# Attention and gated feed-forward on one core: tiles turned one step earlier, query in three parts, normalizing and weight searches at fixed steps, peak sums in the output bank

## Chip, cores, metric

One core of a Trainium2 chip. The time is device time in microseconds (us), lower is better. The engines are TensorE (PE), VectorE (DVE), ScalarE (ACT), GpSimd (POOL) and SyncE (SP); each works through its own queue in order, and they wait for each other by semaphores.

## What is computed

```python
def _A_ref(x, k_cache, v_cache, wq, wo):       # 32 query heads, 16 key/value heads, Dh = 128
    q = (x @ wq).reshape(B, Sq, Hq, Dh).transpose(0, 2, 1, 3)
    k = jnp.repeat(k_cache[:, :, Sk - W:, :], rep, axis=1)    # W = 512, rep = 2
    v = jnp.repeat(v_cache[:, :, Sk - W:, :], rep, axis=1)
    p = _softmax(jnp.einsum("bhqd,bhkd->bhqk", q, k) * (Dh ** -0.5))
    o = jnp.einsum("bhqk,bhkd->bhqd", p, v)
    return o.transpose(0, 2, 1, 3).reshape(B, Sq, Hq * Dh) @ wo
def _B_ref(x, w1, w3, w2):                     # x: 2048 x 576, F = 4608
    return (_silu(x @ w1) * (x @ w3)) @ w2
...
h = _layernorm(x) * (1 + ca) + sa;  x = x + ga * _A_ref(h, ...)
h = _layernorm(x) * (1 + cb) + sb;  x = x + gb * _B_ref(h, ...)
```

The six vectors sa, ca, ga, sb, cb, gb are the parts of silu(c) @ w_mod.

## The kernel before

The order of the instructions on each engine is the order in which the program writes them down; nothing reorders them.

**Slots and steps.** Attention is cut into 128 slots: one query head with one block of 512 rows. Two slots in turn, of the two query heads of one key/value head, form a pair. A key/value head is one "use" of 8 slots (all four blocks) or, for the first three and the last six heads, two uses of 4 slots each, the second of which loads the split weights, keys and values that the first has stored. A slot has four steps, one for each 128 rows. The main loop (L1201 on) runs over slots `i` and steps `t` and writes down, for each step:

- `turn(i - 1, t)` (L406): four PE transposes of a 128 x 512 tile of exponentials into one of two PSUM banks "T", and ACT's copy of the high half into `ptw` (L415);
- `scores(i, t)` (L371): three matmuls (high and low halves in 16 bits), DVE's maximum (L382) and its scaling (L383), then `turn_low(i - 1, t)` (L417, L420, DVE, low half of the turned tile, which frees the bank), then ACT's exponential (L389);
- `sums(i - 1, t)` (L392): the reciprocals of the row sums at step 0, their store to DRAM at step 1, their load, spread over the partitions (`r`), at step 2; store and load are issued by ACT's queue;
- `query(i + 1, t)` (L359): a part of the 14 query matmuls of the next slot; with the last quarter ACT and DVE split the result (L368, L369);
- `attend_out` pieces (L448): six output matmuls into `E`, a tile of two PSUM banks of which 288 columns each are used (L337), and with every second piece DVE's accumulation into `acc` (L453). A pair's eight pieces fill the two slots that begin one slot behind the values of its second slot;
- the tasks that `at` and `step_at` have put down for this step.

Behind step 3 stands `values(i - 1)` (L424): twelve matmuls into `po` (L432), which need all four turned tiles; then, at once, DVE's normalizing with `r` (L436) into `on`, ACT's copy (L445) and POOL's difference (L446).

**Preparing a head.** For each new use, the tasks (L962 on) load keys, values and query weights, search the largest magnitude of each with DVE (`find_peak`, L234), add the peaks over the partitions with one PE matmul against ones and take the powers of two from the sum with DVE (`sum_peaks`, L241; `powers`, L227, its lines 230 to 232), and scale and split them (`split_in` L260, `turn_k` L295, `split_v` L288, `split_out` L277). `sum_peaks` takes one of the two "T" banks. R is the first step of the use; loads are put at R - 22 and R - 21, searches at R - 17 and R - 16, sums at R - 14, splits at R - 13 to R - 11.

**Work for the second stage.** Between slots 13 and 106, POOL and ACT form sums of the feed-forward weights and store them (`make_set` L592, `make_rows` L646, loads `load_raw` L579 and `load_rows` L629, all on SP's queue). Three more modulation vectors are made at slots 14, 20 and 23. From slot 106 on the second layer norm of the first two blocks is formed and stored, read back, combined and stored again as operands of the feed-forward products (`store_h`, `combine`, `load_set` L554). The feed-forward stage, a generator `mlp`, is interleaved with the last slots from slot 127 on and then runs alone: PE multiplies sums of weights with sums of rows (L685) and the results with w2 (L770).

**Buffers.** A pool has a number of buffers for each tag: "T", "A", "S" two PSUM banks each (turned tiles, query and values, scores), `E` one; in SBUF "p" 4, "raw" 3 (raw query weights), "qh" and "ql" 1 each, "kv" 8, "hs" 7, "w" 8, "o" 3.

## Time and profile before

| | us |
|---|---|
| runs | 3148.26, 3139.47, 3142.55 |
| median | 3142.55 |
| profiled execution | 3128.98 |
| its span, first to last instruction | 3127.2 |
| mean granted PE clock in the span | 0.987 |

The profile is of one execution. Busy time of an engine is the time in which one of its instructions ran; matmuls are pipelined, so PE counts as busy also where it runs below its pace. In a timeline row the first number is the start, the second the duration, both in us; x4 joins four instructions; a bracket gives the idle time ahead and what ended it. In a row of waits stand the engine and line that waited, what for, the total, the number of times and the longest.

### The profile page before, as it was taken

How to read it: one execution, taken by the hardware profiler on the slowest of the kernel's cores; microseconds unless marked ns; L12 is line 12 of the kernel's file. 1: busy time of each engine (PE TensorE's matmuls, PEld its weight loads, DVE VectorE, ACT ScalarE, POOL GpSimd, SP SyncE). 2: the span in 40 equal slices, each digit the busy share in tenths (PEclk: the TensorE clock that was granted, in tenths of full speed). 3: DMA queues.
4: the chain of work that ended last, by engine and by line, in shares of the span. 5: the costliest groups of instructions: out<-in, count | busy, mean ns of one | idle time of the engine just before them, and what ended most of it. 6: DMA issues, size and time to landing. Idle time of an engine off the chain costs nothing.

```text
span 3127.2 us, 48547 instructions
## 1 busy us (share of the span) xinstructions
PE 2970.0 (95%) x16952; PEld 2131.3 (68%) x16952; DVE 2050.2 (66%) x3519; ACT 1514.8 (48%) x3077; POOL 1595.2 (51%) x1667
## 2 busy tenths in 40 slices
PE   6899899999999999998999999999999999999999
PEld 3455455555555555555565557888888888888887
DVE  7677567767777777777787666655555555555556
ACT  4566556666666666666655553333333222222222
POOL 2225566666666666666621342435556355343345
PEclk8999899999999999999999999999999999999999
DMA  4325555555555555665632465666766676666664
GB/s 145 104 78 158 161 159 168 157 168 157 158 163 156 161 154 172 213 202 168 211 105 69 143 222 183 202 225 239 247 230 234 229 260 224 198 199 205 195 200 147
DMA packets 336180, 560.53 MB, mean 179 GB/s; under 512 B 51904, under 2 KB 144064, under 8 KB 334144
## 3 DMA queue, kind: packets, MB, share of 16 engines
q1 hardware_dynamic: 298464, 523.59, 50.5%
q10 hardware_dynamic: 37472, 33.84, 4.6%
q8 instruction: 135, 2.21, 0.3%
q14 instruction: 109, 0.89, 0.1%
HBM read 390.92 MB, written 166.36 MB: 178 GB/s over the span
## 4 chain that ended last, share of the span: by engine, by line
PE 66%; DVE 10%; ACT 6%; DMA 6%; POOL 6%; issue 4%; SPq 1%; ACTq 0%; POOLq 0%; DVEq 0%
PE py L685 15%; PE px L685 11%; PE po L432 7%; PE pe L770 6%; PE pf L770 6%; PE pe L337 5%; PE pss L379 5%; PE pq L326 4%; PE pt L414 4%; DVE ptw L420 2%; DVE nm L382 2%; DMA row<-l 2%; ACT ptw L415 2%; DVE on L436 2%; DMA wraw<-in_B_w 1%
## 5 line engine op out<-in xcount | busy, mean ns | idle before, releaser
L389 ACT ACTIVATE p<-pss,nm,factors 128x512 f32<-128x512 f32 x512 | 396.5, 774 | 240.6 <-DVE nm L383 239.5
L685 PE MATMUL py<-hset,wset 128*128 128x512 f32 x2016 | 507.8, 391 | 0.0
L337 PE MATMUL pe<-o 128*128 128x288 f16 x3072 | 459.3, 286 | 17.6 <-DVE acc L453 17.6
L420 DVE SCALAR_TENSOR_TENSOR ptw<-pt,ptw 128x512 f16<-128x512 f32 x512 | 351.1, 686 | 167.7 <-ACT ptw L415 167.5
L382 DVE TENSOR_REDUCE nm<-pss 128x1 f32<-128x512 f32 x512 | 352.0, 688 | 144.6 <-PE pss L379 144.1
L337 PEld LDWEIGHTS <-o 128*128 128x128 f16 x3072 | 299.6, 98 | 194.9 <-issue 33.1
L432 PE MATMUL po<-ptw,v 128*128 128x512 f16 x1536 | 370.2, 386 | 57.7 <-ACT ptw L415 49.2
L379 PE MATMUL pss<-k,qT 128*128 128x512 f16 x1536 | 420.8, 383 | 2.4 <-ACT p L389 1.6
L685 PEld LDWEIGHTS py<-hset,wset 128*128 128x128 f32 x2016 | 362.5, 188 | 59.2
L685 PE MATMUL px<-hset,wset 128*128 128x512 f32 x1512 | 381.0, 391 | 0.0
L414 PE MATMUL pt<-ident,p 128*128 128x128 f32 x2048 | 312.9, 276 | 40.6 <-DVE us L230 28.0
L446 POOL TENSOR_TENSOR o<-on,o 128x512 f16<-128x512 f32 x128 | 148.4, 1159 | 375.0 <-ACT o L445 364.0
L415 ACT ACTIVATE ptw<-pt 128x512 f16<-128x512 f32 x512 | 303.9, 594 | 37.8 <-PE pt L414 27.7
L432 PEld LDWEIGHTS <-v 128*128 128x128 f16 x1536 | 151.8, 99 | 238.2 <-issue 92.5
L685 PEld LDWEIGHTS px<-hset,wset 128*128 128x128 f32 x1512 | 275.5, 188 | 50.0 <-ACT p L389 0.3
L414 PEld LDWEIGHTS pt<-ident,p 128*128 128x128 f32 x2048 | 247.7, 142 | 81.2 <-issue 25.3
L90 POOL TENSOR_TENSOR akv<-u,akv 128x512 fp32r<-128x512 f32 x141 | 181.3, 1294 | 234.8 <-ACT akv L89 232.7
L326 PE MATMUL pq<-hT,wq 128*128 128x512 f16 x1092 | 299.0, 383 | 0.0
L445 ACT CAST o<-on 128x512 f16<-128x512 f32 x128 | 79.1, 618 | 347.9 <-DVE on L436 347.9
L605 POOL TENSOR_TENSOR wmade<-wraw,wmade 128x256 fp32r<-128x256 f32 x252 | 185.2, 735 | 105.0 <-issue 52.0
L453 DVE SCALAR_TENSOR_TENSOR acc<-pe,factors,acc 128x576 f32<-128x576 f32 x256 | 206.9, 808 | 7.3 <-PE pe L337 7.0
L326 PEld LDWEIGHTS <-wq 128*128 128x128 f16 x1104 | 109.3, 99 | 139.6 <-issue 10.3
(186 smaller groups left out, 4907.8 us busy)
## 6 DMA issues: line engine op xcount, KB each, us to landing
oset<-od SPq DMA_DIRECT2D x106, 576.0 KB, 4.8
od<-omade SPq DMA_DIRECT2D x133, 288.0 KB, 3.3
r<-row ACTq DMA_DIRECT2D x128, 256.0 KB, 3.8
wraw<-in_B_w SPq DMA_DIRECT2D x144, 128.0 KB, 2.7
w2raw<-in_B_w SPq DMA_DIRECT2D x38, 288.0 KB, 4.0
oset<-od SPq DMA_DIRECT2D x35, 288.0 KB, 3.3
oraw<-in_A_wo SPq DMA_DIRECT2D x16, 576.0 KB, 6.3
wraw<-in_B_w SPq DMA_DIRECT2D x288, 32.0 KB, 2.4
```

The costliest lines, as they stand in the source:

```text
L326: nc.tensor.matmul(ps, w[:, k // 2, m, :], hT[:, DC + m if k == 1 else m, :], start=s == 0, stop=False)
L337: nc.tensor.matmul(E[:, h, :HALF], o[:, x, rows], w[:, y, h * HALF : (h + 1) * HALF], start=first and n == 0, stop=last and n == 2,)
L379: nc.tensor.matmul(pss, q[:, x, rows], k[:, y, :], start=n == 0, stop=n == 2)
L382: nc.vector.tensor_reduce(nm[:, 0:1], pss, axis=AX.X, op=ALU.max, negate=True)
L389: nc.scalar.activation(p, pss, AF.Exp, bias=nm[:, 1:2], scale=factor, accum_out=st["l"][:, t : t + 1])
L414: nc.tensor.transpose(ps[:, j, :], p[:, j * P : (j + 1) * P], ident)
L415: nc.scalar.activation(st["pt"][:, 0, :, t * P : (t + 1) * P], st["t"], AF.Copy, scale=P_UP)
L420: nc.vector.scalar_tensor_tensor(pt[:, 1, :, cols], state[i]["t"], P_UP, pt[:, 0, :, cols], op0=ALU.mult, op1=ALU.subtract)
L432: nc.tensor.matmul(po, v[:, x, c, :], pt[:, y, c, :], start=c == 0 and n == 0, stop=c == KC - 1 and n == 2)
L453: nc.vector.scalar_tensor_tensor(a, E[:, :, :HALF], factors[:, uses[u][0], 2:3], a, op0=ALU.mult, op1=ALU.add)
L685: nc.tensor.matmul(ps, w[:, a, :], h[:, b, :], start=start and n == 0, stop=stop and n == 6, skip_group_check=True)
L770: nc.tensor.matmul(ps[:, h, :HALF], a[:, rows], w[:, b, :], start=m == 0, stop=m == 2)
```

## The change

- Step `t` of slot `i` turns tile `t + 1` of slot `i - 1`; step 3 turns tile 0 of slot `i` itself. The low half follows behind the scores' maximum, the exponential (now `weights`) behind that.
- The 14 query matmuls are written down as 5, 5 and 4 in steps 0 to 2; the split query takes the tags "qh" and "ql" in turn.
- `values` ends with its matmuls. Normalizing is written down in step 0 of the next slot but one of its own (`normalize(i - 2)`), behind `weights`; copy and difference in step 1 (`split_on`). `on` takes a buffer of "raw".
- The load of `r` stands at the end of step 2, behind that step's tasks.
- Output pieces stand two steps later; those of the last two pairs four and three to a step.
- The sum matmul writes columns 400 to 415 of the second bank of `E`, ahead of the step's output pieces (`("pre", t)`); the reading of the sums (`scales`) is a task of its own one step later.
- The tasks of a head are spread: loads at R - 22 to R - 18, searches at R - 17 and R - 13, sums at R - 10, scales at R - 9, splits at R - 8, R - 4, R - 5 and R - 1; output weights are loaded at R - 3, split at R + 11 and R + 13.
- Weight sums run from slot 16 to 107, loads of w2 rows and their first task two steps earlier; the second layer norm and what follows it one slot later; operands of the products three steps later; two modulation vectors at slots 105 and 108 instead of 20 and 23.

```diff
     def sum_peaks(g, lo, hi, ps=None):
-        ps = t_bank() if ps is None else ps
+        ps = E[:, 1, 400:416] if ps is None else ps
+        nc.tensor.matmul(ps[:, lo:hi], ones, peaks[g][:, lo:hi], start=True, stop=True)
+
+    def scales(g, lo, hi, ps=None):
+        ps = E[:, 1, 400:416] if ps is None else ps
         small = peaks[g]
-        nc.tensor.matmul(ps[:, lo:hi], ones, small[:, lo:hi], start=True, stop=True)
         powers(small, ps, lo, hi, 5, 2.0**-14)
...
-    QP = (range(0, 3), range(3, 6), range(6, 9), range(9, 14))
+    QP = (range(0, 5), range(5, 10), range(10, 14))
...
-            q = st["qT"] = pool.tile([P, 2, SB], F16, tag="qh", name="qT", bufs=QB)
+            q = st["qT"] = pool.tile([P, 2, SB], F16, tag=("qh", "ql")[i % 2], name="qT", bufs=QB)
...
-        on = pool.tile([P, SB], F32, tag="ql", name="on", bufs=QB)
+        st["po"] = po
+
+    def normalize(i):
+        st = state[i]
+        po = st.pop("po")
+        on = st["on"] = pool.tile([P, SB], F32, tag="raw", name="on", bufs=RB)
...
             if pair < n // 2 - 2:
-                when = divmod((2 * pair + 4) * ST + k, ST)
+                when = divmod((2 * pair + 4) * ST + 2 + k, ST)
+            elif pair < n // 2 - 1:
+                when = (n, 2 + k // 4)
             else:
-                when = (pair + n // 2 + 2, k // 2)
+                when = (n + 1, 1 + k // 3)
...
+            A = dict(load=-22, keys=-17, wq=-13, total=-10, scale=-9, put=-8, turn=-5, vals=-1)
+            if u == 1:
+                A.update(load=-16, keys=-13, wq=-13)
+            A = {k: R + v for k, v in A.items()}
...
-        step_at(R + 4, find, wos, u, 4)
-        step_at(R + 6, totals, u, 4, 5)
+        step_at(R + 3 if u else 5, find, wos, u, 4)
+        step_pre(R + 6, totals, u, 4, 5)
+        step_at(R + 7 if u else 7, find_scales, u, 4, 5)
...
-    first_step, last_step = ST * 13, ST * 106
+    first_step, last_step = ST * 16, ST * 107
...
-            lead = 6
+            lead = 6 if maker is make_set else 8
...
-        step_at(ST * (n - 3) + (1, 2, 3, 4, 6, 8, 9)[k], load_set, 0, name)
+        step_at(ST * (n - 2) + (0, 1, 2, 3, 4, 6, 7)[k], load_set, 0, name)
...
-    for i, k in ((14, 5), (20, 3), (23, 4)):
+    for i, k in ((14, 5), (105, 3), (108, 4)):
...
         for t in range(ST):
-            if 1 <= i <= n:
-                turn(i - 1, t)
-            if i == n:
-                turn_low(i - 1, t)
+            slot, tile = (i, 0) if t == ST - 1 else (i - 1, t + 1)
+            if 0 <= slot < n:
+                turn(slot, tile)
             if i < n:
                 scores(i, t)
-            if 1 <= i <= n:
+            if 0 <= slot < n:
+                turn_low(slot, tile)
+            if i < n:
+                weights(i, t)
+            if 1 <= i <= n and t < 2:
                 sums(i - 1, t)
-            if i + 1 < n:
+            if 2 <= i <= n and t == 0:
+                normalize(i - 2)
+            if 2 <= i <= n and t == 1:
+                split_on(i - 2)
+            if i + 1 < n and t < ST - 1:
                 query(i + 1, t)
...
+            run(i, ("pre", t))
             for piece in outs.get((i, t), ()):
                 attend_out(*piece)
             run(i, t)
+            if 1 <= i <= n and t == 2:
+                sums(i - 1, t)
+            run(i, t)
         if 1 <= i <= n:
             values(i - 1)
+        if i == n:
+            normalize(n - 1)
+            split_on(n - 1)
```

More of the change, by code (lines that the diff above doesn't have):

```diff
@@ L365, in query @@
         project(ps, wqs[u, j], hT[b], QP[part])
-        if part == 3:
-            q = st["qT"] = pool.tile([P, 2, SB], F16, tag="qh", name="qT", bufs=QB)
+        if part == len(QP) - 1:
+            q = st["qT"] = pool.tile([P, 2, SB], F16, tag=("qh", "ql")[i % 2], name="qT", bufs=QB)
             nc.scalar.activation(q[:, 0], ps, AF.Copy, scale=Q_DOWN)
@@ L383, in scores, with weights @@
         nc.vector.tensor_scalar(nm[:, 1:2], nm[:, 0:1], factor, None, op0=ALU.mult)
-        if i:
-            turn_low(i - 1, t)
+        st["max", t] = pss, nm
+    def weights(i, t):
+        u, j, b = slots[i]
+        factor = factors[:, uses[u][0], j : j + 1]
+        st = state[i]
+        pss, nm = st.pop(("max", t))
         if t == 0:
@@ L434, in values @@
                 )
-        on = pool.tile([P, SB], F32, tag="ql", name="on", bufs=QB)
+        st["po"] = po
+    def normalize(i):
+        st = state[i]
+        po = st.pop("po")
+        on = st["on"] = pool.tile([P, SB], F32, tag="raw", name="on", bufs=RB)
         nc.vector.scalar_tensor_tensor(
@@ L443, in values, with split_on @@
         )
+    def split_on(i):
+        st = state[i]
+        on = st.pop("on")
         o = st["o"] = pool.tile([P, 2, SB], F16, tag=("ah", "al")[i % 2], name="o", bufs=3)
@@ L914, in scale_gate @@
     def scale_gate():
-        small = odd.tile([P, 16], F32, tag="us", name="us")
-        gate = gates["a"]
-        nc.vector.tensor_reduce(small[:, 0:1], gate, axis=AX.X, op=ALU.max, apply_absolute_value=True)
-        powers(small, small, 0, 1, 5, 2.0)
-        nc.vector.tensor_scalar(gate, gate, small[:, 10:11], None, op0=ALU.mult)
-        nc.vector.tensor_copy(gate_down, small[:, 5:6])
+        small, gate = peaks[0], gates["a"]
+        nc.vector.tensor_reduce(small[:, 4:5], gate, axis=AX.X, op=ALU.max, apply_absolute_value=True)
+        powers(small, small, 4, 5, 5, 2.0)
+        nc.vector.tensor_scalar(gate, gate, small[:, 14:15], None, op0=ALU.mult)
+        nc.vector.tensor_copy(gate_down, small[:, 9:10])
     def find(into, u, k, *key):
@@ L927, in totals, with find_scales @@
         sum_peaks(uses[u][0], lo, hi)
+    def find_scales(u, lo, hi):
+        scales(uses[u][0], lo, hi)
     def put_in(u, j):
@@ L956, in load_made, with step_pre @@
         into[(u, *key) if key else u] = load_kept(kind, (uses[u][0], *key))
+    def step_pre(step, task, *args):
+        at(step // ST, ("pre", step % ST), task, *args)
     def step_at(step, task, *args):
@@ L971, in tile_block @@
         if u:
-            L = max(R - 22, 0)
-            step_at(L, load, keys, u, load_kv, k_cache, g)
-            for j in range(2):
-                step_at(L, load, wqs, (u, j), load_in, wq, (2 * g + j) * DH)
-            step_at(L + 1, load, vals, u, load_kv, v_cache, g)
-            step_at(L + 5, find, keys, u, 2)
-            step_at(L + 5, find, wqs, u, 0, 0)
-            step_at(L + 6, find, wqs, u, 1, 1)
-            step_at(L + 6, find, vals, u, 3)
-            step_at(L + 8, totals, u, 0, 4)
-            step_at(L + 9, put_keys, u)
-            step_at(L + 9, put_in, u, 0)
-            step_at(L + 10, put_in, u, 1)
-            step_at(L + 11, put_values, u)
-            step_at(R - 2, load, wos, u, load_out, g)
-        step_at(R + 4, find, wos, u, 4)
-        step_at(R + 6, totals, u, 4, 5)
+            A = dict(load=-22, keys=-17, wq=-13, total=-10, scale=-9, put=-8, turn=-5, vals=-1)
+            if u == 1:
+                A.update(load=-16, keys=-13, wq=-13)
+            A = {k: R + v for k, v in A.items()}
+            step_at(A["load"], load, keys, u, load_kv, k_cache, g)
+            for j in range(2):
+                step_at(A["load"] + 3 + j if u > 1 else A["load"], load, wqs, (u, j), load_in, wq, (2 * g + j) * DH)
+                step_at(A["wq"], find, wqs, u, j, j)
+                step_at(A["put"] + 4 * j, put_in, u, j)
+            step_at(A["load"] + 2, load, vals, u, load_kv, v_cache, g)
+            step_at(A["keys"], find, keys, u, 2)
+            step_at(A["keys"], find, vals, u, 3)
+            step_pre(A["total"], totals, u, 0, 4)
+            step_at(A["scale"], find_scales, u, 0, 4)
+            step_at(A["turn"], put_keys, u)
+            step_at(A["vals"], put_values, u)
+            step_at(R - 3, load, wos, u, load_out, g)
+        step_at(R + 3 if u else 5, find, wos, u, 4)
+        step_pre(R + 6, totals, u, 4, 5)
+        step_at(R + 7 if u else 7, find_scales, u, 4, 5)
         for j in range(2):
             step_at(R + 5 + j, gate_out, u, j)
-            step_at(R + 9 + j, put_out, u, j)
+            step_at(R + 11 + 2 * j, put_out, u, j)
         if g in again:
@@ L996, in tile_block @@
             step_at(K + 1, keep_made, "w", u, wqs, 1)
-            step_at(K + 2, keep_made, "v", u, vals)
+            step_at(K + 5, keep_made, "v", u, vals)
             step_at(R + 15, keep_made, "o", u, wos)
     last_group = len(groups) - 1
-    first_step, last_step = ST * 13, ST * 106
+    first_step, last_step = ST * 16, ST * 107
     items = []
@@ L1010, in tile_block @@
         if k == 0:
-            lead = 6
+            lead = 6 if maker is make_set else 8
             at((step - lead) // 4, (step - lead) % 4, loader, w)
             if maker is make_rows:
-                at((step - 2) // 4, (step - 2) % 4, maker, w, -1)
+                at((step - 4) // 4, (step - 4) % 4, maker, w, -1)
         at(step // 4, step % 4, maker, w, k)
@@ L1042, in tile_block @@
             at(("m", i), t, load_oset, d, q)
-    for pair, i in ((0, 116), (1, ("m", 14))):
+    for pair, i in ((0, 117), (1, ("m", 14))):
         at(i, 0, split_x, pair)
@@ L1068, in norm @@
             at(i, max(t - 1, 0), norm_rows, b, t)
-    for i, b in ((5, 2), (106, 0)):
+    for i, b in ((5, 2), (107, 0)):
         for k in range(2):
             statistics(i + 2 * k, b + k, 2)
-    for i, b in ((7, 2), (9, 3), (110, 0), (110, 1)):
+    for i, b in ((7, 2), (9, 3), (111, 0), (111, 1)):
         at(i, -1, norm_root, b)
@@ L1091, in combine_parts @@
         combine(pair, c, step, parts[pair])
-    for b, i in ((0, 110), (1, 113)):
+    for b, i in ((0, 111), (1, 114)):
         norm(i, b)
@@ L1096, in tile_block @@
             at(i + 1 + m // 3, m % 3, store_h, b, m, "T", "hf")
-    at(116, -1, begin_parts, 0)
+    at(117, -1, begin_parts, 0)
     for c in range(3):
-        i = 116 + 3 * c
+        i = 117 + 3 * c
         at(i, -1, fill_parts, 0, c)
@@ L1142, in tile_block @@
     at(15, 1, make_gate, "b", 5)
-    at(21, 0, make_cols, "shift", "b", 3, 0.0, "T")
-    at(24, 0, make_cols, "gain", "b", 4, 1.0, "T")
+    at(106, 0, make_cols, "shift", "b", 3, 0.0, "T")
+    at(109, 0, make_cols, "gain", "b", 4, 1.0, "T")
     at(3, -1, load_x, 2)
@@ L1174, in tile_block @@
     scale_cols()
-    sum_peaks(0, 0, 3, E[:, 0, :])
+    sum_peaks(0, 0, 3)
+    scales(0, 0, 3)
     turned.append(turn_rows(0, DC, "S"))
@@ L1184, in tile_block @@
     put_in(0, 1)
-    for part in range(ST):
+    for part in range(len(QP)):
         query(0, part)
@@ L1190, in tile_block @@
     at(0, 3, totals, 0, 3, 4)
+    at(0, 3, find_scales, 0, 3, 4)
     at(1, -1, put_values, 0)
@@ L1203, in tile_block @@
         for t in range(ST):
-            if 1 <= i <= n:
-                turn(i - 1, t)
-            if i == n:
-                turn_low(i - 1, t)
+            slot, tile = (i, 0) if t == ST - 1 else (i - 1, t + 1)
+            if 0 <= slot < n:
+                turn(slot, tile)
             if i < n:
                 scores(i, t)
-            if 1 <= i <= n:
-                sums(i - 1, t)
-            if i + 1 < n:
+            if 0 <= slot < n:
[3 more added lines that the diff above has]
+            if 1 <= i <= n and t < 2:
+                sums(i - 1, t)
+            if 2 <= i <= n and t == 0:
[3 more added lines that the diff above has]
+            if i + 1 < n and t < ST - 1:
                 query(i + 1, t)
```

## The prediction

> **What bounds the kernel now.** I read the page first, then who TensorE (PE) waited for, then the stretches, the timeline of single slots, and last the DMA list.

> ```profile
> span 3127.2 us, 48547 instructions
> ## 1 busy us (share of the span) xinstructions
> PE 2970.0 (95%) x16952; PEld 2131.3 (68%) x16952; DVE 2050.2 (66%) x3519; ACT 1514.8 (48%) x3077; POOL 1595.2 (51%) x1667
> ```

> PE is the bound, but its 95% is a mean over two stages. The next rows cut the span where the feed-forward products begin (the columns are length, then busy time by engine, the granted clock, DMA share and rate):

> ```profile
> 107.60:1880.20 1772.60, 1659.80 (x9846) 1004.04 (x9844) 1277.00 (x2388) 1080.70 (x2319) 991.44 (x1177) 0.99 0.50 156
> 1880.20:3127.20 1247.00, 1239.99 (x6794) 1086.53 (x6791) 699.85 (x970) 382.33 (x666) 573.89 (x456) 1.00 0.64 214
> ```

> In the second stage PE is free for 7 us of 1247: the change can't win there. In attention it is free for 1772.6 - 1659.8 = 112.8 us. The waits of PE over the whole run, in total, times and longest:

> ```profile
> PE po L432 <- ACT ptw L415: 49.2, 36, 4.0
> PE pt L414 <- DVE us L230: 28.0, 31, 3.3
> PE pe L337 <- DVE acc L453: 17.6, 29, 2.0
> ...
> PE pt L140 <- POOL wm L129: 7.3, 1, 7.3
> PE pt L414 <- DVE l L396: 6.5, 8, 1.8
> ```

> Three waits hold most of it. The first is the value product, which waits for the scalar engine's copy of the last turned tile; the second is the turning, which waits until VectorE has read the peak sums out of the bank that it wants; the third is the output product, which waits for its only bank. What a slot costs without waits is read from one undisturbed slot (starts, durations; PE only):

> ```profile
> 1836.23 0.60 PE L414 MATMUL pt<-ident,p 128*128 128x128 f32 x4
> 1836.66 0.81 PE L379 MATMUL pss<-k,qT 128*128 128x512 f16 x3
> 1837.31 0.81 PE L326 MATMUL pq<-hT,w 128*128 128x512 f16 x3
> 1837.96 0.90 PE L337 MATMUL pe<-o 128*128 128x288 f16 x6
> 1838.69 0.60 PE L414 MATMUL pt<-ident,p 128*128 128x128 f32 x4
> ...
> 1846.53 2.75 PE L432 MATMUL po<-ptw,v 128*128 128x512 f16 x12
> 1849.12 0.60 PE L414 MATMUL pt<-ident,p 128*128 128x128 f32 x4
> ```

> From start to start: turning 0.43, scores 0.65, three query products 0.65 (0.216 each), output product 0.73, values 2.59, a step 2.46, the slot 1849.12 - 1836.23 = 12.89 us. How many slots lie in the stretch, and what else PE does there, stands in its groups (count, busy time and mean ns, idle before):

> ```profile
> L414 PE MATMUL pt<-ident,p 128*128 128x128 f32 x1968 | 299.3, 275 | 34.0 <-DVE us L230 26.5 <-DVE l L396 6.5 <-DVE ptw L420 1.1
> ...
> L192 PE MATMUL pt<-ident,xn 128*128 128x128 f32 x80 | 12.1, 273 | 0.0
> L299 PE MATMUL pt<-ident,kvraw 128*128 128x128 f32 x56 | 8.4, 273 | 0.0
> L245 PE MATMUL pt<-us,ones 128*128 128x1 f32 (+1 forms) x58 | 8.2, 212 | 0.0
> L140 PE MATMUL pt<-ones,wm 128*128 128x1 f32 (+1 forms) x48 | 6.1, 269 | 7.3 <-POOL wm L129 7.3
> ```

> 1968 transposes at 16 a slot are 123 slots: 123 x 12.89 = 1585.5 us. With 34.8 us of the other groups and 112.8 us free, 1772.6 - 1585.5 - 34.8 - 112.8 = 39.5 us are left, in which PE counts as busy and runs slower than in the quiet slot. What that is shows behind a stall of 0.86 us, and in the granted clock (seventh column of the stretches) of the next 3 us, beside the quiet slot's:

> ```profile
> 1277.32 0.90 PE L414 MATMUL pt<-ident,p 128*128 128x128 f32 x4 [0.86 <-DVE us L230]
> ```
> ```profile
> 1278.00:1281.00 3.00, 3.00 (x10) 1.08 (x8) 1.36 (x3) 0.85 (x3) 1.65 (x3) 0.51 0.40 107
> ...
> 1836.00:1849.00 13.00, 13.00 (x80) 7.98 (x79) 9.36 (x17) 8.05 (x17) 11.20 (x9) 1.00 0.52 158
> ```

> A stall can halve the clock for about 3 us. [...]

> **The change part by part.** No instruction of the slots is added or taken away; they are placed elsewhere in five in-order queues.

> *Tiles turned one step ahead (values no longer wait for the tile turned in their own step).* The case at 965 us shows what was waited for: the scalar engine stands for 4 us at the issue of the store of the row sums.

> ```profile
> 960.53 0.19 ACT L389 ACTIVATION_READ_ACCUMULATOR p<-pss,nm,factors 128x1 f32 x1
> 964.87 0.34 ACTq L399 DMA_DIRECT2D row<-l  x1
> 965.30 0.43 ACT L640 CAST omade<-w2raw 128x288 fp32r<-128x288 f32 x1 [4.58 <-DMA wraw<-in_B_w]
> 965.64 0.59 ACT L415 ACTIVATE ptw<-pt 128x512 f16<-128x512 f32 x1
> ...
> 967.83 0.59 ACT L415 ACTIVATE ptw<-pt 128x512 f16<-128x512 f32 x1
> ```
> ```profile
> 968.47 1.75 PE L432 MATMUL po<-ptw,v 128*128 128x512 f16 x6 [2.94 <-ACT ptw L415]
> ```

> Values need the copy of 967.83; after the edit they need the one before it, of 965.64, 2.2 us earlier. The stop of ACT stays (the store is issued at the same step), but 2.94 us become 0.8. The 36 waits have a mean of 1.37 us: most vanish. I keep 5 of 49.2 us: **-44**. Bounds: 0 (the stop moves with the lead) to 49.2. The row store keeps its step, the load of the reciprocals goes behind its step's tasks, and the exponentials behind the turned tile's low half, as before. The tile turned in step 3 is the new slot's first, written three steps earlier; the four buffers of p still hold.

> *Peak sums in the spare columns of the output bank.* The turning no longer waits for VectorE (DVE) to empty its bank. The sum matmul stands ahead of the step's output product, at the third step of a slot, its reading one step later, behind the accumulation and ahead of the values: until the next output product PE has 2.59 + 0.43 + 0.65 + 1.08 = 4.75 us of other work, DVE one accumulation (0.81 us, below) and the reading, of which the turning in the row above saw 0.86 us. If DVE is over 3 us late there, that cover is gone and the wait returns under another name. I take 27 of 28.0: **-27**, bounds 0 to 28.0.
> [...]

> *Query in three steps, outputs two steps later, searches at the fourth step.* The query's 14 products fall as 5, 5, 4: steps are 2.9, 2.9, 2.7, then 1.8 with values of 2.6 behind it. DVE's accumulation is one operation of

> ```profile
> L453 DVE SCALAR_TENSOR_TENSOR acc<-pe,factors,acc 128x576 f32<-128x576 f32 x256 | 206.9, 808 | 7.3 <-PE pe L337 7.0
> ```

> 0.81 us, and PE's work until it wants the bank again grows from 0.43 + 0.65 + 0.65 = 1.73 us to 2.16 us behind the second step, and is 4.75 us behind the fourth, where the searches and sums now stand. **-12** of 17.6; bounds +5 (a late DVE) to -17.6. Normalizing moves from behind the values into the next step 0, behind the scores' maximum: DVE stops waiting for PE there. By the stretch, DVE has 1277.0 / 123 = 10.4 us of work a slot, ACT 8.8, POOL 8.1, against 12.89: none becomes the bound by its sum. Its result takes one of the three buffers of the raw weights, two of which wait 11 and 14 steps for their splitting; the one left must be free after four steps, 12.9 us, which POOL has to spare: 0. Query tiles get two buffers for one: 0, for scores hardly waited.

> *Loads.* Keys, values and the two query weights of a head (8 DMAs) go from two steps to four, its output weights one step earlier, the kept values three later; two of the modulation loads (4 DMAs), with their weighing on DVE, ACT and POOL, go from slots 19 and 22 to 104 and 107. SP passes them among the same weight loads, no sooner wanted by PE. Of the 7.3 + 6.5 us of the last two waits I take **-4**, bounds 0 to -13.8.

> *Seam to the second stage.*

> ```profile
> r<-row ACTq DMA_DIRECT2D x128, 256.0 KB, 3.8
> ...
> hset<-hd0p SPq DMA_DIRECT2D x7, 1280.0 KB, 10.8
> ```

> The first product operand is now loaded four steps ahead of its use instead of seven: one slot, 12.9 us, against 10.8 us to land: +2, bounds 0 to +15 (seven sets). The last two pairs' outputs stand four or three to a step; four times one follows the accumulation of the other in the one bank, at about 1 us: +4, bounds 0 to +8. The start I leave at 0, bounds -10 to +5: DVE holds it before and after.

> *Slower running.* 44 + 27 + 12 + 4 = 87 of 112.8 us free time go, some of it outside the stretch; in proportion 0.7 x 39.5: **-28**, bounds 0 to -39.5.
> [...]

> **Sum.** 44 + 27 + 12 + 4 + 28 - 2 - 4 = 109 us. The profiled execution took 3128.98 us (span 3127.2): it would be 3020. It lies 13.6 us below the median of the runs shown, 3142.55, from which the same 109 give **3033.5 us**, 3.5% less.

> **The rivals.**
> 1. *The stops move.* ACT still stands at its two DMA issues of each slot, and DVE behind it; values lose only half their wait and the clock its share. For it: the 4.58 us above. Against it: the lead of a step. The gain halves to 55: 3088.
> 2. *The slow part stays.* If the 39.5 us have another cause than short stalls, 109 - 28 = 81 are won: 3061. [...]
> 3. *The output bank takes over the wait.* PE waits for the reading of the sums at the output product instead of the turning: 27 us less won, and the clock's share of it, about 9: 3070. Against it: 4.75 us of cover.
> 4. *No change, the turning ahead does nothing.* If ACT and DVE run a step late everywhere, not in single stops, the lead is used up at once: none of the 44, the 12 and their clock; the 27 are spent at the bank (rival 3) and the seam: 3142 within 9. Against it: ACT is free for 4 of 12.9 us.
> 5. *Slower: normalizing waits for the reciprocals.* Their load is now issued behind the query's split on ACT, and DVE, in order, stands at normalizing with the maximum, the low half and the accumulation of the next step queued behind it, and the exponentials and the output product behind those. From the query's end to normalizing lie 0.73 + 1.8 + 2.6 + 1.1 on PE and two DVE operations, some 7.6 us; the load lands in 3.8. It decides from an issue 3.8 us behind the query's end, and has eaten the whole gain at 0.9 us beyond that in each of 123 slots; 1.1 us give 3169. For it: ACT stops of 4 us. Against it: they come in some slots, not in each.

> **How the numbers follow.** Forecast (gain 90 to 147): 0.65. Rival 1: 0.13; rival 2: 0.09; rival 3: 0.05; rival 4: 0.03; rival 5: 0.05. A measurement of this kernel tells about 0.3%, 9 us, from no change. Faster is the sum of the forecast and the first three rivals, 0.92; same 0.03; slower 0.05. The range goes down to 3142.55 - 147 = 2995 (waits of 49.2 + 28.0 + 17.6 + 13.8 and 38 of slow running, nothing lost) and up past rival 1 to 3090; what lies outside, rivals 4 and 5 and the tails of the others, is some 0.15.

> **What would show it.** Right: "po <- ptw" under 10 us, "pt <- us" gone with no "pe <- us" in its place, "pe <- acc" under 8, free PE time in attention near 30 us, the slot's median at 12.9, the mean clock of the stage nearer 1.00. Wrong: "on" waiting for "r" on DVE (rival 5), a wait of output products for DVE's reading of the sums (rival 3), free time gone but the clock as it was (rival 2), ACT's waits for DMA grown and "po" still late (rival 1), py or px waiting for hset at the seam.

## The result, and the profile after

The changed kernel takes 3025.07 us (median of four runs, 3023.43 to 3027.85) against 3145.41 us of the kernel before: ratio 0.962, 95% interval 0.960 to 0.964. In a later session of five rounds it was 3022.06 against 3139.86, ratio 0.9633 (0.9615 to 0.9652).

The profiled execution's page after, its head:

```profile
span 3021.6 us, 48488 instructions
## 1 busy us (share of the span) xinstructions
PE 2937.5 (97%) x16952; PEld 2125.7 (70%) x16952; DVE 2030.5 (67%) x3519; ACT 1521.3 (50%) x3077; POOL 1588.1 (53%) x1667
```

The span is 105.6 us shorter. The same cut as before, from the start of slot 4 (slots are counted from 0) to the step of the first feed-forward product (length, then busy time by engine, granted clock seventh):

```profile
100.80:1761.50 1660.70, 1624.99 (x9834) 996.79 (x9832) 1258.54 (x2389) 1087.55 (x2319) 985.39 (x1177) 1.00 0.54 165
1761.50:3021.60 1260.10, 1244.61 (x6802) 1089.00 (x6799) 700.19 (x972) 383.21 (x668) 573.54 (x456) 1.00 0.65 215
```

The 123 slots went from 1772.6 to 1660.7 us, 111.9 less. The start, 107.6 before, is 6.8 us shorter. The rest is 13.1 us longer. 111.9 + 6.8 - 13.1 = 105.6. PE's free time in the slots fell from 112.8 to 1660.7 - 1625.0 = 35.7 us. PE's waits after, over the whole run:

```profile
PE po L442 <- ACT ptw L425: 14.3, 9, 2.8
PE pe L341 <- DVE acc L472: 12.7, 16, 1.9
PE pt L192 <- DVE xn L182: 9.9, 1, 9.9
PE pe L244 <- DVE acc L472: 5.0, 7, 1.4
...
PE pt L140 <- POOL wm L129: 2.8, 2, 1.4
```

The line numbers moved: L442 is the old L432, L341 the old L337, L424 the old L414, L472 the old L453, and L244 is the sum matmul. The values wait 9 times instead of 36; the turning no longer waits for the peak sums (`us`); the sum matmul now waits 5.0 us for the accumulation.

The slow running can be worked out as the prediction did. The four small groups that the prediction took out (a fifth, of 2.2 us in both kernels, is left out in both) took

```profile
L192 PE MATMUL pt<-ident,xn 128*128 128x128 f32 x80 | 12.1, 273 | 0.2 <-ACT hf L204 0.2
L244 PE MATMUL pe<-us,ones 128*128 128x1 f32 (+1 forms) x58 | 8.6, 233 | 5.1 <-DVE acc L472 5.0
L303 PE MATMUL pt<-ident,kvraw 128*128 128x128 f32 x56 | 8.4, 273 | 1.2 <-issue 1.2
L140 PE MATMUL pt<-ones,wm 128*128 128x1 f32 (+1 forms) x48 | 5.1, 244 | 2.8 <-POOL wm L129 2.8
```

34.2 us, and 1660.7 - 123 x 12.89 - 34.2 - 35.7 = 5.3 us are left, against 39.5 before.

The longer rest has two places that the trace shows, at the seam between the stages, where the kernel before had no such waits. PE's waits from 1761.5 to 1830 us:

```profile
PE pe L341 <- DVE acc L472: 4.7, 5, 1.4
PE pss L383 <- ACT p L399: 3.5, 1, 3.5
```

The second goes back to one late load of the reciprocals (starts, durations, in brackets the idle time ahead):

```profile
1762.04 0.33 ACTq L412 DMA_DIRECT2D r<-row  x1
1762.46 1.96 PE L706 MATMUL py<-hset,wset 128*128 128x512 f32 x7
...
1769.98 1.05 DVE L451 SCALAR_TENSOR_TENSOR on<-po,r 128x512 f32<-128x512 f32 x1 [3.99 <-DMA r<-row]
...
1772.89 1.44 PE L383 MATMUL pss<-k,qT 128*128 128x512 f16 x3 [3.51 <-ACT p L399]
1773.77 3.55 PE L706 MATMUL py<-hset,wset 128*128 128x512 f32 x7
```

DVE stands 4 us at normalizing, the maximum and the exponential are late behind it, and PE stops for 3.5 us. From 1771.6 to 1778.4 us the granted clock is 0.5: three matmuls take 1.44 us instead of 0.81, seven feed-forward products 3.55 instead of 1.96, and from start to start the half clock costs some 2.6 us up to 1778.49. This is the chain that rival 5 feared, once. The load landed 7.8 us after its issue, against a median of 3.8; why is not shown. About 1.0 us of the 13.1 is only moved: two output pieces of 0.73 us now stand behind the cut, and one turned tile of 0.43 us ahead of it. 4.7 + 3.5 + 2.6 + 1.0 = 11.8; what remains, about 1 us, is not accounted for.

### The profile page after: what moved, and what is told of

It is laid out like the page before. It is cut to its first block, busy times and chain, and to the rows that moved or that the text cites. A ratio compares the mean times of both kernels' runs of the same rounds, so it can differ in the third digit from the quotient of the medians.

```text
span 3021.6 us, 48488 instructions
## 1 busy us (share of the span) xinstructions
PE 2937.5 (97%) x16952; PEld 2125.7 (70%) x16952; DVE 2030.5 (67%) x3519; ACT 1521.3 (50%) x3077; POOL 1588.1 (53%) x1667
## 5 line engine op out<-in xcount | busy, mean ns | idle before, releaser
L399 ACT ACTIVATE p<-pss,nm,factors 128x512 f32<-128x512 f32 x512 | 397.4, 776 | 391.3 <-DVE nm L387 390.3
L341 PE MATMUL pe<-o 128*128 128x288 f16 x3072 | 460.9, 287 | 13.1 <-DVE acc L472 12.7
L341 PEld LDWEIGHTS <-o 128*128 128x128 f16 x3072 | 300.7, 99 | 183.0 <-issue 23.9
L442 PE MATMUL po<-ptw,v 128*128 128x512 f16 x1536 | 354.8, 379 | 15.6 <-ACT ptw L425 14.3
L424 PE MATMUL pt<-ident,p 128*128 128x128 f32 x2048 | 309.1, 274 | 9.2 <-ACT hf L204 4.5
L330 PE MATMUL pq<-hT,wq 128*128 128x512 f16 x1092 | 282.2, 381 | 1.2 <-DVE hT L202 1.2
L424 PEld LDWEIGHTS pt<-ident,p 128*128 128x128 f32 x2048 | 249.1, 141 | 46.6 <-ACT hf L204 4.7
L442 PEld LDWEIGHTS <-v 128*128 128x128 f16 x1536 | 150.2, 98 | 177.0 <-issue 22.2
L472 DVE SCALAR_TENSOR_TENSOR acc<-pe,factors,acc 128x576 f32<-128x576 f32 x256 | 207.6, 811 | 27.5 <-PE pe L341 27.0
L383 PEld LDWEIGHTS <-qT 128*128 128x128 f16 x1536 | 150.8, 98 | 73.1 <-issue 5.3
## 6 DMA issues: line engine op xcount, KB each, us to landing
r<-row ACTq DMA_DIRECT2D x128, 256.0 KB, 3.8
```

What stands on the lines that cost most here:

```text
L330: nc.tensor.matmul(ps, w[:, k // 2, m, :], hT[:, DC + m if k == 1 else m, :], start=s == 0, stop=False)
L341: nc.tensor.matmul(E[:, h, :HALF], o[:, x, rows], w[:, y, h * HALF : (h + 1) * HALF], start=first and n == 0, stop=last and n == 2,)
L383: nc.tensor.matmul(pss, q[:, x, rows], k[:, y, :], start=n == 0, stop=n == 2)
L399: nc.scalar.activation(p, pss, AF.Exp, bias=nm[:, 1:2], scale=factor, accum_out=st["l"][:, t : t + 1])
L424: nc.tensor.transpose(ps[:, j, :], p[:, j * P : (j + 1) * P], ident)
L442: nc.tensor.matmul(po, v[:, x, c, :], pt[:, y, c, :], start=c == 0 and n == 0, stop=c == KC - 1 and n == 2)
```

## The experiments

**Theory at the outset:** the waits that went were single stops; the lead of a step hides them, the output bank takes the sums, and each wait takes its share of halved clock along; the parts add up. **Rivals:** the stops only move (1), the bank takes over the wait (3), the load of the reciprocals comes too late (5).

Ratios are against the kernel before, in the same rounds on the same chip.

| run | median us | before | ratio (95%) |
|---|---|---|---|
| turning alone | 3118.23 | 3143.56 | 0.9918 (0.9899 to 0.9938) |
| sums alone | 3142.92 | 3143.56 | 0.9994 (0.9985 to 1.0003) |
| turning and query | 3094.08 | 3139.31 | 0.9853 (0.9833 to 0.9874) |
| change, turning undone | 3172.91 | 3143.56 | 1.0089 (1.0071 to 1.0107) |
| change, sums undone | 3048.39 | 3143.56 | 0.9689 (0.9673 to 0.9706) |
| change, head tasks undone | 3061.79 | 3139.31 | 0.9761 (0.9742 to 0.9781) |
| change, normalizing undone | 3054.34 | 3139.31 | 0.9729 (0.9714 to 0.9743) |
| change, load of r undone | 3048.39 | 3139.86 | 0.9711 (0.9696 to 0.9727) |
| change again | 3022.06 | 3139.86 | 0.9633 (0.9615 to 0.9652) |
| change, loads spread | 3012.22 | 3139.31 | 0.9596 (0.9581 to 0.9610) |
| the same and the seam mended | 3008.45 | 3139.86 | 0.9587 (0.9571 to 0.9604) |

### One part alone

**The turning alone**, on the kernel before:

```diff
-            if 1 <= i <= n:
-                turn(i - 1, t)
...
+            slot, tile = (i, 0) if t == ST - 1 else (i - 1, t + 1)
+            if 0 <= slot < n:
+                turn(slot, tile)
             if i < n:
                 scores(i, t)
+            if 0 <= slot < n:
+                turn_low(slot, tile)
+            if i < n:
+                weights(i, t)
```

> The kernel before with the turning one step ahead and nothing else. Theory (the lead covers ACT's stops, and the clock goes with the waits): the wait of the value product for ACT falls from 49 us to under 15, free PE time in attention from 113 to about 75, and the time by 45 to 55 us, to 3090 to 3100. Rival 1 (the stops move): ACT still stops as long, and the value product keeps half its wait; 15 to 25 us less, 3120 to 3130. If the turning ahead only works together with the query in three steps, nothing changes: 3140 to 3150.

Measured: 3118.23, 25 us less, by its time nearest to rival 1. But rival 1's mechanism did not happen. PE's waits in this run:

```profile
PE pe L337 <- DVE acc L459: 33.7, 42, 1.5
PE pt L420 <- DVE us L230: 28.7, 31, 3.4
PE pt L420 <- DVE l L402: 16.4, 16, 4.6
PE pss L379 <- ACT qT L368: 14.7, 13, 2.1
...
PE po L438 <- ACT ptw L421: 2.5, 2, 1.5
```

The wait of the values is gone almost wholly, 49.2 to 2.5 us, more than the prediction had hoped. In its place the output product waits 33.7 us for the accumulation (17.6 before), the turning 16.4 for l (6.5), and the scores 14.7 for the split of the query, for which they had hardly waited. 41 of the 47 us came back at three other places. The likely reason, which no run isolates, is that DVE and ACT had caught up with PE while it stood ahead of the values, and now they do not.

**The sums alone**, on the kernel before:

```diff
-        ps = t_bank() if ps is None else ps
+        ps = E[:, 1, 400:416] if ps is None else ps
...
-            step_at(L + 8, totals, u, 0, 4)
+            step_pre(L + 8, totals, u, 0, 4)
+            step_at(L + 9, find_scales, u, 0, 4)
```

> The kernel before with the peak sums in the spare columns of the output bank, read one step later, and nothing else. Theory (27 us of waits and their share of the slow clock): the turning's wait for us goes, 28 us, and 30 to 40 us in all, to 3105 to 3115. Rival 3 (the output bank takes over the wait): a wait of the sums or of the output product for DVE of 20 us or more in its place, and a time within 10 us of 3145.

Measured: no change (0.9994). The waits tell where the 28 us went:

```profile
PE po L436 <- ACT ptw L419: 68.2, 47, 4.0
PE pe L244 <- DVE acc L457: 20.0, 17, 2.0
PE pe L341 <- DVE acc L457: 10.9, 11, 1.7
```

Rival 3 is right here: the sum matmul waits 20.0 us for the accumulation, though that reads columns 0 to 287 of each bank and the sums go to columns 400 to 415 of the second. And the values wait 68.2 us for ACT (49.2 and 57.7 in the two profiles of the kernel before).

So the waits do not add up. From here the theory was: they stand one behind the other, and a part that takes one away is worth only what the next in line leaves.

**Turning and query in three steps**, on the turning alone (with the query's second buffer, for which `on` moves to the raw weights' buffers):

```diff
-    QP = (range(0, 3), range(3, 6), range(6, 9), range(9, 14))
+    QP = (range(0, 5), range(5, 10), range(10, 14))
...
-            if i + 1 < n:
+            if i + 1 < n and t < ST - 1:
                 query(i + 1, t)
```

> The kernel before with the turning one step ahead and the query in three steps (with the two query buffers that this needs). New theory (the waits stand one behind the other: behind the one that is taken away the next comes up): with the turning alone the scores waited 14.7 us for the split of the query and the output product 33.7 us for the accumulation; the first goes, the second, DVE's, stays at 25 to 35 us, and the time is 10 to 20 us below the turning alone, 3098 to 3108. Old theory (the parts add up): 3118 less the query's own worth of nothing, 3115 to 3120.

Measured: 3094.08, a little better than the range; by the ratios 0.9918 - 0.9853 = 0.65%, 20 us. The scores' wait for the query fell from 14.7 to 5.2 us, that of the output product from 33.7 to 25.7. The turning waits as long as before, 29.0 us for the low half where it was 28.7 us for the peak sums (`us`):

```profile
PE pt L420 <- DVE ptw L426: 29.0, 29, 3.2
PE pe L337 <- DVE acc L459: 25.7, 33, 1.8
PE pt L420 <- DVE l L402: 15.8, 13, 4.3
...
PE pss L379 <- ACT qT L368: 5.2, 8, 1.1
```

The prediction had the scores' wait at nothing, and in the kernel before it was 0.7 us; the turning alone had opened it. This wait is 9.5 us shorter, the output product's 8.0.

### One part undone

**The turning undone**, in the changed kernel:

```diff
-            slot, tile = (i, 0) if t == ST - 1 else (i - 1, t + 1)
+            slot, tile = i - 1, t
```

> The changed kernel with the tile turned in its own step again, everything else as changed. Theory: the fourth step is now short (1.8 us), so the values stand closer behind the last tile's copy than in the kernel before and wait in most slots, not in one of four: 60 to 120 us more, 3085 to 3145. If the turning were worth only what the single stops cost: 40 to 50 us more, 3065 to 3075. If it did nothing: 3025.

Measured: 3172.91, 148 us above the changed kernel and above the kernel before. The values wait in most slots now:

```profile
PE po L442 <- DVE ptw L430: 75.9, 110, 1.8
PE po L442 <- ACT ptw L425: 73.2, 54, 6.2
```

The theory's direction holds and its range was too low. The query in three steps makes the fourth step short, so without the lead the values stand closer behind their last tile, as the rows show. The query in three steps needs the turning ahead.

**The sums undone**, in the changed kernel:

```diff
     def find_scales(u, lo, hi):
-        scales(uses[u][0], lo, hi)
+        ps = t_bank()
+        sum_peaks(uses[u][0], lo, hi, ps)
+        scales(uses[u][0], lo, hi, ps)
...
-            step_pre(A["total"], totals, u, 0, 4)
```

> The changed kernel with the peak sums in a bank of the turning again, summed and read at the step where the changed kernel reads them. Theory: 28 to 35 us more, 3053 to 3060, with the wait of the turning for us back at 25 to 30 us. If the place of the searches, now three steps ahead of the sums, had already removed that wait: under 10 us more, 3025 to 3035.

Measured: 3048.39, some 18 to 23 us above the changed kernel (by the ratios 0.6 to 0.7%), under the range. The expected wait of the turning for `us`, 25 to 30 us, did not come back; in its place the sum matmul waits 17.9 us for its bank, and the clock is lower (0.988 in the span, against 0.991). The same part was worth nothing alone.

**The tasks of a head undone**: loads, searches, scales and splits at the old steps, the sums still in the output bank.

```diff
-            A = dict(load=-22, keys=-17, wq=-13, total=-10, scale=-9, put=-8, turn=-5, vals=-1)
...
+            step_at(L + 5, find, keys, u, 2)
+            step_at(L + 5, find, wqs, u, 0, 0)
+            step_at(L + 6, find, wqs, u, 1, 1)
+            step_at(L + 6, find, vals, u, 3)
+            step_pre(L + 8, totals, u, 0, 4)
+            step_at(L + 9, find_scales, u, 0, 4)
```

> The changed kernel with the tasks of a head (loads, searches, scales, splits) at the steps of the kernel before, and all the rest as changed. New theory (DVE's lateness by the searches is what the output product and the sums wait for): the waits for the accumulation and for l, ptw and us rise from 20 us to 45 to 65 us, and the time by 35 to 60 us, to 3060 to 3085. If the turning ahead and the three query steps are enough alone: under 10 us more, 3025 to 3035.

Measured: 3061.79, about 42 us above the changed kernel by the ratios, at the lower end of the range. The waits for the accumulation, l, ptw and `us` rose to 39 us, less than the 45 to 65 expected. The sum matmul waits 14.7 us for the accumulation again (5.0 in the changed kernel), and the values wait 19.0 us for ACT (14.3):

```profile
PE po L442 <- ACT ptw L425: 19.0, 9, 4.4
PE pe L244 <- DVE acc L472: 14.7, 14, 2.4
```

So the heads' tasks separate the sums alone from the sums in the change. In this trace a search of some 1.3 us, or two of 0.7 to 0.8 us, stands on DVE within 7 us ahead of each of these 14 waits; that the searches alone are the cause is not shown, since the run undid loads and splits with them.

**Normalizing undone**, right behind the values again:

```diff
-            if 2 <= i <= n and t == 0:
-                normalize(i - 2)
-            if 2 <= i <= n and t == 1:
-                split_on(i - 2)
...
         if 1 <= i <= n:
             values(i - 1)
+            normalize(i - 1)
+            split_on(i - 1)
```

> The changed kernel with normalizing right behind the values again, and copy and difference behind it. New theory: DVE then stands for the values in each slot, about 1 us by the idle time of DVE ahead of on in the kernel before, and the accumulation and the maximum behind it are late: 10 to 30 us more, 3035 to 3055. If DVE has slack enough: within 5 us, 3020 to 3030.

Measured: 3054.34, 30 us above the changed kernel by the ratios, at the upper end. The reason given was only half right. DVE does stand there, but most of all for the reciprocals; first the rows of this run, then those of the changed kernel (idle time of DVE ahead of normalizing, times):

```profile
  DMA r<-row: 38.4, 27
  PE po L442: 15.0, 20
```
```profile
  DMA r<-row: 5.1, 2
  PE po L442: 2.2, 1
```

**The load of r undone**, issued ahead of the query's split and the step's tasks again:

```diff
-            if 1 <= i <= n and t < 2:
+            if 1 <= i <= n and t < 3:
                 sums(i - 1, t)
...
-            if 1 <= i <= n and t == 2:
-                sums(i - 1, t)
-            run(i, t)
```

(The last line found no task left to run.)

> The changed kernel with the load of the reciprocals at its old place, behind the step's exponential and ahead of the query's split. Theory (ACT stops at that issue for the row store, and what stands behind it is late): the split of the query and the tasks of the third step are late, DVE waits for them: 3 to 15 us more than the changed kernel, with DVE's wait for r unchanged near 5 us. Rival 5 in its weak form (the later issue costs something): 3 to 10 us less. Otherwise within 3 us.

Measured: 3048.39 against 3022.06 of the changed kernel in the same rounds, 26 us more, beyond what was expected. DVE waits for ACT's half of the query's split; this run, then the changed kernel:

```profile
DVE qT L373 <- ACT qT L372: 181.7, 127, 6.1
```
```profile
DVE qT L373 <- ACT qT L372: 95.7, 127, 2.4
```

ACT waits at that issue for the row store and for weight loads (37.5 and 19.2 us of its idle time ahead of the split), and what is written down behind it waits with it: 86 us more of DVE's idle time, and the accumulation late behind that (22.2 us of waits of the output product, 12.7 in the changed kernel). DVE's wait for r itself was 4.6 us, against 5.1 in the changed kernel: the later issue adds next to nothing to it. Rival 5 is not only wrong; the step that it feared is a gain.

### The rest of ACT's stops, and the seam

ACT's stops at its DMA issues did not shrink with the change; their main rows before and after (in all 88 us in the slots before, 99 after):

```profile
ACT omade L640 <- DMA wraw<-in_B_w: 19.3, 9, 4.6
ACT wmade L604 <- DMA wraw<-in_B_w: 16.2, 7, 2.9
ACT wmade L604 <- DMA row<-l: 14.4, 9, 3.5
```
```profile
ACT o L464 <- DMA wraw<-in_B_w: 42.4, 17, 5.4
ACT ptw L425 <- DMA wraw<-in_B_w: 21.0, 8, 3.9
ACT ptw L425 <- DMA row<-l: 20.4, 13, 3.4
```

PE's wait for ACT fell from 49.2 to 14.3 us all the same: the lead hides the stops, it doesn't remove them. That much of the first theory is shown.

**The loads spread**, in the changed kernel: the twelve loads of a block of weights in four steps instead of one.

```diff
-            at((step - lead) // 4, (step - lead) % 4, loader, w)
+            if maker is make_set:
+                for part in range(4):
+                    at((step - lead + part) // 4, (step - lead + part) % 4, loader, w, part)
+            else:
+                at((step - lead) // 4, (step - lead) % 4, loader, w)
```

> The changed kernel with the twelve loads of a block of feed-forward weights issued in four steps instead of one. ACT's stops at its DMA issues are waits for such loads (42.4, 21.0 and 20.4 us in the changed kernel). If these come from the burst of twelve, the stops fall to less than half, the value product's remaining wait from 14 to under 6 us, and the time by 8 to 15 us, to 3010 to 3017. If the stops come from the DMA engines' load itself: 3020 to 3030, and the stops stay.

Measured: 3012.22, ratio 0.9596, some 12 us below the changed kernel's 0.9633. The stops for weight loads fell to a third (63.4 to 20.5 us); those for the row store, which were expected to fall too, did not:

```profile
ACT ptw L425 <- DMA row<-l: 26.3, 16, 3.9
...
ACT o L464 <- DMA wraw<-in_B_w: 10.9, 5, 3.5
ACT ptw L425 <- DMA wraw<-in_B_w: 9.6, 5, 2.6
```

The values' wait is 5.9 us. So the burst was the cause of most of the first kind of stops, and only of that.

Why a store of 2 KB issued by ACT waits for loads issued by SP stands in the semaphore fields of the traces. The program's 2184 DMAs share eight semaphores, 273 each, and in both kernels none was issued before the DMA ahead of it on its semaphore had landed (2176 pairs in each trace, the closest 16 ns apart). In the kernel before, the store of 964.87 us has the semaphore of the weight load that SP issued at 962.46 and that landed at 964.85. The twelve loads of a block take all eight semaphores in 66 of the 72 blocks of the two traces and seven in the others. The stop at the load of r is of another kind: it waits for the store whose row it reads. In the changed kernel one such store was issued at 233.92 and landed at 237.20, and the load followed at 237.22. Spreading the weight loads did not remove that stop: the turned tile's copy waits 26.3 us for the row store with it, 20.4 without.

**The seam mended**, on top of that: output pieces by two with products between, the product operands two steps earlier.

```diff
-                when = (n, 2 + k // 4)
+                when = ((n, 2), (n, 3), (n + 1, 0), (n + 1, 0))[k // 2]
...
-                when = (n + 1, 1 + k // 3)
+                when = (n + 1, (1, 2, 3, 3)[k // 2])
...
-        step_at(ST * (n - 2) + (0, 1, 2, 3, 4, 6, 7)[k], load_set, 0, name)
+        step_at(ST * (n - 2) + (-2, -1, 0, 1, 2, 4, 5)[k], load_set, 0, name)
```

> The changed kernel with the loads spread (as in the run before it) and the seam mended: the last two pairs' output pieces by two, with products between them, and the product operands loaded two steps earlier. Theory (the seam lost 4.7 us to the one output bank and some 6 us to a late load of the reciprocals, which the operand loads crowd, with its half clock): 5 to 9 us below the loads spread alone on the same footing, 13 to 22 us below the changed kernel. If the seam's loss has another place: within 3 us of the loads spread alone, 9 to 14 us below the changed kernel.

Measured: 3008.45, 13.6 us below the changed kernel in the same rounds (0.9587 against 0.9633, intervals apart): the fastest version of this study. Against the loads spread alone the ratios are 0.9587 and 0.9596 with intervals that overlap: the 5 to 9 us of the theory did not come, and the seam's own worth isn't shown to be more than noise. The output product's wait did fall (12.4 us with the loads spread, 8.4 now); the stop of 3.5 us for the exponential stayed, so earlier operand loads do not cure it; the load of r at that place still took 8.3 us to land.

### The two kernels again

> The changed kernel unaltered, on the chip and in the rounds of the others: the footing for runs that differ by less than 1%. 3015 to 3030; in its profile the waits of PE within 10 us of the first profile's, the attention stretch within 10 us of 1661.

Measured: 3022.06; span 3018.4, slots 1658.6 us, the waits of the values 13.7 us (14.3 in the first profile).

> The kernel before unaltered, for a second profile. The first profiled execution lay 16 us below the median of the runs, so the sum of the terms and the difference of the medians differ by that much. If single executions differ by where PE's stalls fall in the clock's rhythm, this profile shows 10 to 20 us more than 3127 in the attention stretch, as waits and half clock; if the profile itself makes the kernel faster, it is again near 3127.

Measured: 3139.97 in the runs; this profile's span is 3142.4 us, the slots 1786.0 (1772.6 in the first), the values' wait 57.7 us (49.2). Of the 13.4 us between the two, 8.5 lie in the values' wait, and the time at half clock in the slots is 61.4 us instead of 44.4: single executions of the kernel before differ by their stops, and the first profile was a quick one. That is the larger part of why the spans differ by 105.6 us and the medians by 120. With the second profiles the spans' means are 3134.8 and 3020.0, 114.8 apart.

## Why the prediction was right, and where not

The forecast was 3033.5 us, a gain of 109; measured are 3025.07 and 120 by the medians, 105.6 by the first profiles. By its own steps:

- **PE is the bound, and only attention can win: right.** The slots gave 111.9 us, about 1.0 of it work that now stands behind the cut.
- **Turning ahead, -44:** the wait fell by 35 us in the change, to 14.3 us; the prediction had kept 5 and gave under 10 as its sign. The mechanism (a stop of ACT stays, the lead hides it) is shown by the rows of ACT. As a term on its own it was wrong: alone it gave 25 us, of 47 us of waits removed.
- **Sums in the output bank, -27:** 28.0 us went and 5.0 came back. Alone it gave nothing, as rival 3 had it; in the change, undone, it costs 18 to 23.
- **The accumulation, -12:** 17.6 to 12.7 us, 4.7 of these new at the seam.
- **Loads and layer norms, -4:** 13.8 to 4.8 us, twice as good.
- **Slower running, -28:** 39.5 to 5.3 us, -34. It went with the stops, so rival 2 is out. By the clock records the slots ran 44.4 us at half clock before and 10.2 after, an estimated loss of half of that, 22 and 5 us (seven feed-forward products took 3.55 us at half clock instead of 1.96). The other 17 us that went are no half clock, and what they are is not shown. A value product right behind a stop took 2.88 us from start to start at full clock (844.29 to 847.17) instead of 2.59; there its third matmul started at 845.02, behind DVE's low half of 844.27 to 844.96, a wait that counts as busy. The proportion of slow running to waits was the author's estimate, which no run isolates. That a stop of 0.86 us halves the clock by itself was misread (last section).
- **Seam, +6:** 13.1 us, of which about 1.0 only moved. The waits of about 1 us for the one output bank came, five instead of four (4.7); no product waited for its operands; the late load of r at that place, with its half clock some 6 us, was not foreseen there.
- **Start, 0:** 6.8 us less; the cause is open.
- **The step that failed is "costed at nothing":** the query's gain at the scores and the later normalizing were put at 0, and the later load of r stands in no term, as moves of work that nothing waits for. Undone or added one at a time the query in three steps is worth 20 us, the other two 30 and 26. The sum came out right because the waits that the prediction wrote off mostly go when all parts are in; the division among the parts was wrong, and neither part that was tried alone earned its own term.
- **Some of it is luck.** The four terms of waits gave 72 us instead of 87 and the seam cost 7 more, while the slower running gave 6 and the start 7 more than said. That these nearly cancel was not foreseen.

Left open: which engine's lateness is behind each wait that comes up, why one load of r took twice as long at the seam, and what the seam's last microsecond is.

## What to carry to other kernels

A wait row of the bound engine was not the price of the wait here: with the turning alone 47 us of one row went and the time fell by 25, since the lateness of other engines was the next row. So ask of each wait that is to go which engine will be late next, and by how much it is late already; and try a schedule as a whole before its parts are thrown out one by one, since here one part alone was worth nothing and another about half of its row. The load of r, on which ACT stops, was worth 26 us behind the work that others wait for. The burst of twelve weight loads on SP held up the issues of ACT, which share the eight semaphores with them: ACT's stops for weight loads fell from 63.4 to 20.5 us when it was spread.

## What the runs showed of the hardware

The prediction showed a clock of 0.51 behind a stop of 0.86 us. In the same stretch lay another stop, of 1.21 us. PE was free for 3.40 - 1.33 = 2.07 us of it, and the next stretch ran at 0.50:

```profile
1275.45 0.90 PE L337 MATMUL pe<-o 128*128 128x288 f16 x6 [1.21 <-DVE acc L453]
```
```profile
1274.10:1277.50 3.40, 1.33 (x11) 1.00 (x10) 3.05 (x8) 2.64 (x6) 2.17 (x5) 1.00 1.01 367
1277.50:1280.90 3.40, 3.40 (x11) 1.52 (x10) 1.86 (x4) 0.75 (x2) 2.05 (x3) 0.50 0.38 103
```

In the changed kernel a stop of 2.84 us lay across the border of two stretches. PE was free for 1.65 us of the one and 1.33 us of the other, and the clock stayed up:

```profile
844.29 3.04 PE L442 MATMUL po<-ptw,v 128*128 128x512 f16 x12 [2.84 <-ACT ptw L425]
```
```profile
839.70:843.10 3.40, 1.75 (x13) 1.08 (x12) 0.00 (x0) 1.98 (x4) 1.16 (x1) 1.00 0.61 144
843.10:846.50 3.40, 2.07 (x9) 0.87 (x9) 1.67 (x3) 2.71 (x7) 3.34 (x4) 1.00 0.57 138
846.50:849.90 3.40, 3.40 (x21) 2.01 (x20) 3.12 (x7) 2.17 (x5) 0.98 (x2) 1.00 0.78 222
```

Counted over the slots of all 14 traces, for the stretches of 3.41 us that ran at full clock:

| PE free in the stretch, us | stretches | next one at half clock |
|---|---|---|
| under 1 | 6533 | 8 |
| 1 to 1.75 | 251 | 10 |
| 1.75 to 2 | 40 | 17 |
| over 2 | 69 | 68 |

In the two first profiles alone the rows are 938 and 1, 38 and 2, 4 and 1, 8 and 8. So a short stop alone cost no clock here (none of 138 stops of 0.5 to 1 us with no other stop within 7 us halved it); stops of 1.21 and 0.86 us in one stretch, above, stood ahead of half clock.

**Of the 18 cases in the first two rows of the table, 17 are stretches with ten or more products with one output column.** They are the 128x1 products of the modulation vectors (L140), and they count as busy; why half clock follows them is not shown. In the changed kernel's slots all the half clock that is left, 10.2 us from 1478.0 and 1525.8 us on, stands behind two such stretches, with 15 and 22 of these products and PE free for 1.37 and 0.24 us.
